# Weight loads on GpSimd's queue, earlier value loads, and the low-rank first half moved inside its pair, in a fused attention and MLP kernel

## The chip, the cores and the metric

The kernel runs on one core of a Trainium2 chip. The metric is device time in microseconds (us), from start to end of one execution. A core has five engines with queues of their own that work in order and wait for one another through semaphores: TensorE (PE, matrix products), VectorE (DVE), ScalarE (ACT), GpSimd (POOL) and SyncE (SP). Here SyncE computes nothing; it starts DMA transfers, each an instruction in its queue. ScalarE and GpSimd can start transfers too.

## The reference

Attention with a sigmoid in place of the softmax, over 4 batches and 12 heads, then two mixing blocks on the joined heads:

```
scores = q @ k.T / sqrt(64) - log(448);  attn = sigmoid(scores);  x = attn @ v     # per head, 448 x 64
h = x.T @ U @ V;  u = x + h.T                                                      # U 448 x 32, V 32 x 448
x = u + relu(u @ w_ch1) @ w_ch2                                                    # 768 -> 3072 -> 768
theta = x @ w_theta;  y = w_tok_r @ (x * cos(theta)) + w_tok_i @ (x * sin(theta))
u = x + y;  out = u + relu(u @ w_ch)
```

The inputs of attention are 32-bit floats; U, V and the weights are 64-bit floats, which the kernel loads as pairs of 32-bit words and turns into 32-bit floats itself. Most factors are split into a rounded high part and the remainder, and a product is taken as hi·hi + hi·lo + lo·hi.

## The kernel before

**Attention** is the first stage. It takes two heads of one batch at a time: 24 pairs, numbered p = 0 to 23, six to a batch. The loop is at lines 614 to 658, and its text is the order of the instructions on every engine. In one pass over p TensorE does the score products of p in three chunks of 128 keys (`QK`, tile `sc`, line 404) and the value products of pair p-1 (`AV`, tile `av`, line 430, and `AV_rest`, line 442). ScalarE turns a chunk of scores into weights (tile `A`, `AL` for the last 64 keys, line 395). VectorE transposes and splits the queries and keys of p+1 (`TK`, `TQ`, `K_lo`). `XN` transposes the finished x of pair p-2 back (tile `xt`, line 454) and VectorE copies it to the tile `xn` (line 455). `xn` has one buffer, so the first copy of a batch must wait until the batch before has been read out of it. The scores have two PSUM buffers: the chunk after the next must wait until ScalarE has read this one.

**The low-rank term.** `U1(b)` multiplies U with the batch's `xn` (tile `p`, line 464, 12 products in the program, 24 rows in the trace), and ScalarE and VectorE split the result into `pc`. `U2_one` (lines 608 to 612, 487) multiplies `pc` by `vcat`, the split of V, and VectorE adds the product `h` to x (line 493). `pc` and `vcat` stack their parts along the 128 rows of the contraction, 32 rows each. U1 for batches 0, 1 and 2 is issued at p = 8, 14 and 20 (lines 644 to 647), and U2 runs twice a pass in the three passes that follow. U1 for batch 3 comes after attention (line 716).

**Loads.** Queries and keys (`load_qk`, four transfers of 56 KB for each tile) are asked for four pairs ahead, values (`load_v`: one of 384 KB and two of 32 KB, for two pairs) at the end of each even pass, for the two pairs from p+2. A value tile has two buffers. All of these are in SyncE's queue, but for pair 0's queries and first values, which ScalarE starts. Each transfer uses one of eight completion semaphores in turn, and an issue waits for the transfer that had the semaphore before, so at most eight are under way in SyncE's queue.

**Converting the 64-bit weights.** A `Conv` job (lines 124 to 162) loads words to a tile `ws` (three buffers, 768 KB for a weight tile), then takes five steps on ScalarE and VectorE, and its first step asks for the load of the job after the next. Nine jobs run inside attention, two steps a pass (`early_step`): w1, U, V for even and odd batches, then six more weight tiles. Their loads are in SyncE's queue where the program text comes to them.

**After attention** come the two large products in 12 blocks of 4 batches (`ch1`, `ch2`), the token mixing and the last product. From the end of the first block's second batch (line 778) `late["sp"]` is set, and the low part of a weight is then made by GpSimd and not by VectorE.

Of the kernel before, what the change touches and what calls it, by code (L numbers as in the profile page):

```python
# [24 lines left out]
def tile_kernel(  # L25
# [156 lines left out]
    def fin_split(dest, key, name, tag):  # L182
        def fin(a, t):
            dest[key] = ring(tag, name)
            split(dest[key], a, lo_dve if late.get("sp") is None else lo_pool)
        return fin

    def load_row(src, r0):
        def dma(s):
            nc.sync.dma_start(out=s.rearrange("p n t -> p (n t)"), in_=src[r0:r0 + P, :])  # L190
        return dma

    def conv_w1(i, j):
        c0 = (i * FB + j) * P

        def dma(s):
            nc.sync.dma_start(
                out=s.rearrange("p (k f) t -> p k (f t)", k=NK),
                in_=w1_w[:, 2 * c0:2 * (c0 + P)].rearrange("(k p) f -> p k f", p=P),
            )  # L200
        return Conv(f"w1_{i}_{j}", P, DM, dma, fin_split(w1_t, (i, j), f"w1_{i}_{j}", "w1"))
# [69 lines left out]
    def conv_U():  # L271
        def dma(s):
            sv = s.rearrange("p (a c r) t -> p a c (r t)", a=2, c=NC)

            def put(o, i):
                nc.sync.dma_start(out=o, in_=i)

            for par in range(2):
                for c0, n0, n1 in ((0, 0, P), (1, P, NFULL * P), (NFULL, S - P, S)):
                    for n, t, m in runs(par, n0, n1):  # L280
                        if m > P:
                            put(sv[:, par, c0:NFULL], U_w[t:t + m, :].rearrange("(c p) w -> p c w", p=P))
                        else:
                            put(sv[n - n0:n - n0 + m, par, c0], U_w[t:t + m, :])

        def dest():
            return u_in.rearrange("p a c r -> p (a c r)").bitcast(U32)
        return Conv("U", P, 2 * NC * R, dma, None, dest=dest)

    def conv_V(par):  # L290
        def dma(s):
            sv = s.rearrange("r n t -> r (n t)")
            for n, t, m in runs(par, 0, S):
                nc.sync.dma_start(out=sv[:, 2 * n:2 * (n + m)], in_=V_w[:, 2 * t:2 * (t + m)])

        def fin(a, t):
            o = vcat[:, par]
            for g in (0, 2):
                hi_act(o[g * R:(g + 1) * R], a)
                lo_dve(o[(g + 1) * R:(g + 2) * R], a, o[:R])  # L300
        return Conv(f"V{par}", R, S, dma, fin)
# [11 lines left out]
    u_in = ap.tile([P, 2, NC, R], F32, name="u_in")  # L313
    vcat = ap.tile([P, 2, S], F32R, name="vcat")

# [143 lines left out]
    def U1(b, p):  # L459
        ps = ps_a.tile([P, 512], F32, tag="ux", name=f"p1_{b}")  # L460
        for c in range(NC):
            r = slice(P - REM if c == NFULL else 0, P)
            for g in range(3):
# [3 lines left out]
                )  # L467
        o = p.tile([P, DM], F32R, tag="pc", name=f"pc_{b}")
        for g in range(3):
# [7 lines left out]
    def u1_lo():  # L477

        while u1_t:
            ps, o = u1_t.pop()  # L480
            for g in range(3):
                x = ps[g * R:(g + 1) * R, :2 * P]
                sl = slice(2 * g * P, 2 * (g + 1) * P)
                for m in range(2):
                    lo_dve(o[(2 + m) * R:(3 + m) * R, sl], x, o[:R, sl])

# [127 lines left out]
    for p in range(NP):  # L614
# [13 lines left out]
        if nx:  # L628
            K_lo(p + 1)
        U2_one(p, 0)  # L630
        QK(p, 2)
# [10 lines left out]
        if p % 2:  # L642
            AV_rest(p // 2)
        b, r = divmod(p - 2 - NH, NH)
        if b >= 0 and r == 0:
            U1(b, ap)
        u1_lo()
        U2_one(p, 1)
        if p in (4, 6):
            early_step()  # L650
        if p + 4 < NP:
            load_qk(p + 4)
        if p % 2 == 0 and p + 2 < NP:
            load_v(p // 2 + 1)
        if p == 0:
# [53 lines left out]
    uv, uv_st = pool("uv", "right")  # L709
    vlast = uv.tile([P, S], F32R, name="vlast")  # L710
    split_u(1, u01, 0, NK, lo_pool, lo_dve)
# [293 lines left out]
```

## Time and profile before

| | |
|---|---|
| median of 3 runs | 1198.64 us (1196.73 to 1199.26) |
| the profiled execution's own time | 1195.74 us |
| its span, first to last instruction | 1194.0 us |
| busy, PE / DVE / ACT / POOL | 1173.7 / 651.2 / 366.2 / 155.7 us |
| weight loads `ws_w`, median from issue to landing | 4.5 us for 768 KB |
| `k` and `q` loads on SyncE, the same | 2.5 and 2.3 us for 56 KB |

Attention ends at about 184 us. The busy times are shares of the whole span; what a wait costs is read from the stage in which it lies. Matrix products overlap, so a product's own length is not its cost: the distance between starts is. The chain of waits gives such distances for TensorE while it is the engine that ends last. An instruction's bracket in the timeline says how long its engine was idle before it and what ended that.

### The profile page before, as it was taken

The page shows a single profiled execution, that of the slowest core. Times are in us where ns is not written, and L with a number is a line of the kernel's source. Part 1 is how long each engine was busy: PE and PEld are TensorE (multiplying, and loading weights), DVE is VectorE, ACT ScalarE, POOL GpSimd, SP SyncE. Part 2 cuts the span into 40 slices and gives each one's busy share as a digit, 9 for nine tenths or more (in the row PEclk, how much of TensorE's full clock was granted, in tenths as well). Part 3 has the DMA queues.
Part 4 walks back from the last instruction along what each step waited for, and adds up shares of the span by engine and source line. Part 5 has one row for each costly group of instructions (what it writes and reads, how often), then busy time and mean ns, then how long its engine had stood idle before and what let it go on. Part 6 is the DMA issues. An engine that isn't in the chain of part 4 may idle for free.

```text
span 1194.0 us, 15048 instructions
## 1 busy us (share of the span) xinstructions
PE 1173.7 (98%) x6172; PEld 1005.7 (84%) x6172; DVE 651.2 (55%) x828; ACT 366.2 (31%) x482; POOL 155.7 (13%) x94
## 2 busy tenths in 40 slices
PE   8899989999999999999999999999999999999998
PEld 4434437999999999999999999999989999999997
DVE  5676865455555555555546565656454642833443
ACT  6667665211122211221212121212124431631110
POOL 0000001411111111111111111212002421320000
PEclk9999999999999999999999999999999999999999
DMA  7687630011222122212222241415242000040344
GB/s 140 143 162 163 116 90 1 27 53 54 84 95 96 53 84 95 95 56 82 95 95 73 75 148 54 159 53 185 110 157 80 1 1 1 3 158 1 52 65 69
DMA packets 177988, 99.18 MB, mean 83 GB/s; under 512 B 140064, under 2 KB 170048, under 8 KB 177792
## 3 DMA queue, kind: packets, MB, share of 16 engines
q1 hardware_dynamic: 152976, 94.79, 28.0%
q10 hardware_dynamic: 24944, 3.44, 2.0%
q8 instruction: 48, 0.79, 0.3%
q14 instruction: 20, 0.16, 0.0%
HBM read 80.05 MB, written 18.15 MB: 82 GB/s over the span
## 4 chain that ended last, share of the span: by engine, by line
PE 94%; DMA 2%; DVE 1%; SPq 1%; issue 0%; ACT 0%; ACTq 0%; DVEq 0%
PE y L698 10%; PE g L676 10%; PE y L700 10%; PE g L678 10%; PE g L677 10%; PE y L699 10%; PE av L430 4%; PE sc L404 3%; PE y L887 3%; PE y L888 3%; PE y L886 3%; PE th L809 2%; PE th L813 2%; PE th L810 2%; PE wc L968 2%; PE wc L969 2%
## 5 line engine op out<-in xcount | busy, mean ns | idle before, releaser
L702 DVE TENSOR_TENSOR X<-y,X 128x896 f32<-128x896 f32 x144 | 157.1, 1091 | 113.3 <-PE y L700 111.8
L698 PE MATMUL y<-gh,w 128*128 128x448 f32 x576 | 211.6, 367 | 0.0
L676 PE MATMUL g<-uh,w 128*128 128x448 f32 x576 | 211.1, 367 | 0.0
L677 PE MATMUL g<-ul,w 128*128 128x448 f32 x576 | 210.9, 366 | 0.0
L700 PE MATMUL y<-gh,w 128*128 128x448 f32 x576 | 210.9, 366 | 0.0
L678 PE MATMUL g<-uh,w 128*128 128x448 f32 x576 | 210.9, 366 | 0.0
L699 PE MATMUL y<-gl,w 128*128 128x448 f32 x576 | 210.8, 366 | 0.0
L683 ACT ACTIVATE gh<-g 128x896 fp32r<-128x896 f32 x48 | 44.1, 919 | 414.9 <-PE g L678 414.9
L684 DVE SCALAR_TENSOR_TENSOR gl<-g,gh 128x896 fp32r<-128x896 f32 x48 | 52.4, 1091 | 190.7 <-ACT gh L683 190.7
L112 POOL TENSOR_TENSOR w<-ca_w,w 128x768 fp32r<-128x768 f32 x42 | 77.8, 1853 | 497.0 <-ACT w L109 497.0
L676 PEld LDWEIGHTS g<-uh,w 128*128 128x128 f32 x576 | 108.2, 188 | 9.7 <-issue 0.4
L698 PEld LDWEIGHTS y<-gh,w 128*128 128x128 f32 x576 | 108.2, 188 | 9.6 <-issue 0.4
L700 PEld LDWEIGHTS y<-gh,w 128*128 128x128 f32 x576 | 108.2, 188 | 9.5
L678 PEld LDWEIGHTS g<-uh,w 128*128 128x128 f32 x576 | 108.2, 188 | 9.4
L677 PEld LDWEIGHTS g<-ul,w 128*128 128x128 f32 x576 | 108.2, 188 | 9.2
L699 PEld LDWEIGHTS y<-gl,w 128*128 128x128 f32 x576 | 108.2, 188 | 9.1
L395 ACT ACTIVATE A<-sc,bias_s 128x896 f32<-128x896 f32 x72 | 69.8, 1004 | 22.9 <-PE sc L404 22.6
L430 PE MATMUL av<-A,v 128*64 128x448 f32 x288 | 65.5, 563 | 4.1 <-DMA v<-in_v_dram 4.1
L886 PE MATMUL y<-tok,zh 128*128 128x448 f32 x168 | 61.7, 367 | 0.0
L887 PE MATMUL y<-tok,zh 128*128 128x448 f32 x168 | 61.5, 366 | 0.0
L888 PE MATMUL y<-tok,zl 128*128 128x448 f32 x168 | 61.4, 366 | 0.0
L109 ACT ACTIVATE w<-ca_w 128x768 fp32r<-128x768 f32 x48 | 40.3, 839 | 63.8 <-PE y L700 63.8
(132 smaller groups left out, 1619.1 us busy)
## 6 DMA issues: line engine op xcount, KB each, us to landing
ws_w<-in_moe_w_ch_dram SPq DMA_DIRECT2D x48, 768.0 KB, 4.5
k<-in_k_dram SPq DMA_DIRECT2D x96, 56.0 KB, 2.5
q<-in_q_dram SPq DMA_DIRECT2D x92, 56.0 KB, 2.3
ws_th<-in_moe_w_theta_dram SPq DMA_DIRECT2D x6, 768.0 KB, 4.2
th_d<-sp_th SPq DMA_DIRECT2D x6, 768.0 KB, 4.2
ws_wc<-in_moe_w_ch_dram SPq DMA_DIRECT2D x6, 768.0 KB, 4.7
wc_d<-sp_wc SPq DMA_DIRECT2D x6, 768.0 KB, 4.1
th_r<-th_d SPq DMA_DIRECT2D x6, 768.0 KB, 5.3
```

The costliest lines, as they stand in the source:

```text
L112: nc.gpsimd.tensor_sub(o, a, b)
L430: nc.tensor.matmul(ps[h * D:(h + 1) * D, :S], v_t[p // 2][:, 2 * (p % 2) + h, c, :], A_t[p, c][:, h, :], start=c == 0 and p % 2 == 0, stop ...
L676: nc.tensor.matmul(o, wh[:, sl], uh_t[b][:, kk, :], start=kk == 0, stop=False)
L677: nc.tensor.matmul(o, wh[:, sl], ul_t[b][:, kk, :], start=False, stop=False)
L678: nc.tensor.matmul(o, wl[:, sl], uh_t[b][:, kk, :], start=False, stop=kk == NK - 1)
L698: nc.tensor.matmul(o, wh[:, sl], gh[:, j, :], start=j == 0, stop=False)
L699: nc.tensor.matmul(o, wh[:, sl], gl[:, j, :], start=False, stop=False)
L700: nc.tensor.matmul(o, wl[:, sl], gh[:, j, :], start=False, stop=j == FB - 1)
L702: nc.vector.tensor_add(x, ps[:, :, :S], x)
L886: nc.tensor.matmul(o, zh[:, sl], tok_h[:, i, :], start=n == 0, stop=False)
L887: nc.tensor.matmul(o, zh[:, sl], tok_l[:, i, :], start=False, stop=False)
L888: nc.tensor.matmul(o, zl[:, sl], tok_h[:, i, :], start=False, stop=n == NZ - 1)
```

## The change

All loads of `Conv` jobs inside attention (weights, U, V) are issued by GpSimd in place of SyncE; after line 778's point they are on SyncE as before. `load_v` stands ahead of `load_qk` at the end of an even pass. `U1` and `u1_lo` move from the end of passes 8, 14 and 20 into their middle, between `K_lo` and the first `U2_one`. `pc` and `vcat` lose their fourth 32 rows: the contraction runs over hi·hi, lo·hi and hi·lo (96 rows) and no longer over lo·lo, and for each batch VectorE makes three low parts of `pc` in place of six, and for each of two V tiles one low part in place of two.

```diff
--- before.py
+++ after.py
@@ -182,19 +182,22 @@
     def fin_split(dest, key, name, tag):
         def fin(a, t):
             dest[key] = ring(tag, name)
-            split(dest[key], a, lo_dve if late.get("sp") is None else lo_pool)
+            split(dest[key], a, lo_pool if "sp" in late else lo_dve)
         return fin
+
+    def loader():
+        return nc.sync if "sp" in late else nc.gpsimd
 
     def load_row(src, r0):
         def dma(s):
-            nc.sync.dma_start(out=s.rearrange("p n t -> p (n t)"), in_=src[r0:r0 + P, :])
+            loader().dma_start(out=s.rearrange("p n t -> p (n t)"), in_=src[r0:r0 + P, :])
         return dma
 
     def conv_w1(i, j):
         c0 = (i * FB + j) * P
 
         def dma(s):
-            nc.sync.dma_start(
+            loader().dma_start(
                 out=s.rearrange("p (k f) t -> p k (f t)", k=NK),
                 in_=w1_w[:, 2 * c0:2 * (c0 + P)].rearrange("(k p) f -> p k f", p=P),
             )
@@ -273,7 +276,7 @@
             sv = s.rearrange("p (a c r) t -> p a c (r t)", a=2, c=NC)
 
             def put(o, i):
-                nc.sync.dma_start(out=o, in_=i)
+                nc.gpsimd.dma_start(out=o, in_=i)
 
             for par in range(2):
                 for c0, n0, n1 in ((0, 0, P), (1, P, NFULL * P), (NFULL, S - P, S)):
@@ -291,13 +294,13 @@
         def dma(s):
             sv = s.rearrange("r n t -> r (n t)")
             for n, t, m in runs(par, 0, S):
-                nc.sync.dma_start(out=sv[:, 2 * n:2 * (n + m)], in_=V_w[:, 2 * t:2 * (t + m)])
+                nc.gpsimd.dma_start(out=sv[:, 2 * n:2 * (n + m)], in_=V_w[:, 2 * t:2 * (t + m)])
 
         def fin(a, t):
             o = vcat[:, par]
             for g in (0, 2):
                 hi_act(o[g * R:(g + 1) * R], a)
-                lo_dve(o[(g + 1) * R:(g + 2) * R], a, o[:R])
+            lo_dve(o[R:2 * R], a, o[:R])
         return Conv(f"V{par}", R, S, dma, fin)
 
     cv, cv_st = pool("cv")
@@ -311,7 +314,7 @@
     ps_a, ps_a_st = pool("ps_a", "left", PSUM)
     ps_b, ps_b_st = pool("ps_b", "right", PSUM)
     u_in = ap.tile([P, 2, NC, R], F32, name="u_in")
-    vcat = ap.tile([P, 2, S], F32R, name="vcat")
+    vcat = ap.tile([3 * R, 2, S], F32R, name="vcat")
 
     vl_t, AL_t = {}, {}
     q_t, k_t, v_t, qq_t, kk_t, A_t, av_t, xn_t = {}, {}, {}, {}, {}, {}, {}, {}
@@ -465,7 +468,7 @@
                     ps[g * R:(g + 1) * R, :2 * P], u_in[r, b % 2, c, :], xn_t[b][r, c, 2 * g * P:2 * (g + 1) * P],
                     start=c == 0, stop=c == NC - 1,
                 )
-        o = p.tile([P, DM], F32R, tag="pc", name=f"pc_{b}")
+        o = p.tile([3 * R, DM], F32R, tag="pc", name=f"pc_{b}")
         for g in range(3):
             x = ps[g * R:(g + 1) * R, :2 * P]
             sl = slice(2 * g * P, 2 * (g + 1) * P)
@@ -481,8 +484,7 @@
             for g in range(3):
                 x = ps[g * R:(g + 1) * R, :2 * P]
                 sl = slice(2 * g * P, 2 * (g + 1) * P)
-                for m in range(2):
-                    lo_dve(o[(2 + m) * R:(3 + m) * R, sl], x, o[:R, sl])
+                lo_dve(o[2 * R:, sl], x, o[:R, sl])
 
     def U2(b, d, ps, vc, n=1):
         for m in range(n):
@@ -627,6 +629,10 @@
             early_step()
         if nx:
             K_lo(p + 1)
+        b, r = divmod(p - 2 - NH, NH)
+        if b >= 0 and r == 0:
+            U1(b, ap)
+            u1_lo()
         U2_one(p, 0)
         QK(p, 2)
         if not nx:
@@ -641,17 +647,13 @@
             AV(p - 1, 2)
         if p % 2:
             AV_rest(p // 2)
-        b, r = divmod(p - 2 - NH, NH)
-        if b >= 0 and r == 0:
-            U1(b, ap)
-        u1_lo()
         U2_one(p, 1)
         if p in (4, 6):
             early_step()
+        if p % 2 == 0 and p + 2 < NP:
+            load_v(p // 2 + 1)
         if p + 4 < NP:
             load_qk(p + 4)
-        if p % 2 == 0 and p + 2 < NP:
-            load_v(p // 2 + 1)
         if p == 0:
             seq[1].load()
         if p:
@@ -707,7 +709,7 @@
         AV(NP - 1, c)
     ap1_st.close()
     uv, uv_st = pool("uv", "right")
-    vlast = uv.tile([P, S], F32R, name="vlast")
+    vlast = uv.tile([3 * R, S], F32R, name="vlast")
     split_u(1, u01, 0, NK, lo_pool, lo_dve)
     XN(NP - 2)
     ch1(0, 0)
```

SyncE's queue from pair 2's queries on. First before, then now; the first number in a name is the pair (`k_3`) or the pair of passes (`v_1` holds the values of pairs 2 and 3).

```order
L327 DMA q_2_127<-in_q_dram 32x14x32 x4
L197 DMA ws_w1_0_0_136<-in_moe_w_ch1_dram 128x6x256
L327 DMA k_3_138<-in_k_dram 32x14x32 x4
L327 DMA q_3_139<-in_q_dram 32x14x32 x4
L327 DMA k_4_243<-in_k_dram 32x14x32 x4
L327 DMA q_4_244<-in_q_dram 32x14x32 x4
L349 DMA v_1_253<-in_v_dram 128x4x192
L354 DMA vl_1_254<-in_v_dram 64x2x64 x2
L276 DMA ws_U_258<-in_moe_U_dram 128x64
L276 DMA ws_U_258<-in_moe_U_dram 128x2x64
L276 DMA ws_U_258<-in_moe_U_dram 128x64
L276 DMA ws_U_258<-in_moe_U_dram 64x64 x2
```

```order
L330 DMA q_2_127<-in_q_dram 32x14x32 x4
L330 DMA k_3_138<-in_k_dram 32x14x32 x4
L330 DMA q_3_139<-in_q_dram 32x14x32 x4
L352 DMA v_1_243<-in_v_dram 128x4x192
L357 DMA vl_1_244<-in_v_dram 64x2x64 x2
L330 DMA k_4_248<-in_k_dram 32x14x32 x4
L330 DMA q_4_249<-in_q_dram 32x14x32 x4
L330 DMA k_5_322<-in_k_dram 32x14x32 x4
L330 DMA q_5_323<-in_q_dram 32x14x32 x4
L352 DMA v_2_394<-in_v_dram 128x4x192
L357 DMA vl_2_395<-in_v_dram 64x2x64 x2
L330 DMA k_6_399<-in_k_dram 32x14x32 x4
```

The weight load behind `q_2` and the U loads are gone, and each `v` stands ahead of two query and key tiles that it stood behind. On GpSimd, which before did nothing between making the identity and its first subtraction after attention, the weight load of the first job is now the next instruction behind the identity, with U and V behind it:

```order
masks.py:197 MEMSET ident_63 128x128
masks.py:199 ISA
masks.py:199 AFFINE_SELECT ident_63<-ident_63 128x128
L200 DMA ws_w1_0_0_136<-in_moe_w_ch1_dram 128x6x256
L279 DMA ws_U_258<-in_moe_U_dram 128x64
L279 DMA ws_U_258<-in_moe_U_dram 128x2x64
L279 DMA ws_U_258<-in_moe_U_dram 128x64
L279 DMA ws_U_258<-in_moe_U_dram 64x64 x2
L279 DMA ws_U_258<-in_moe_U_dram 128x2x64
L279 DMA ws_U_258<-in_moe_U_dram 128x64
L297 DMA ws_V0_300<-in_moe_V_dram 32x896
```

ScalarE in pass 8 and the beginning of pass 9, before and now:

```order
L395 ACTIVATE A_8_0_799<-sc_8_0_792,bias_s_64 128x896
L395 ACTIVATE A_8_1_808<-sc_8_1_801,bias_s_64 128x896
L109 ACTIVATE kh_9_823<-kT_9_810 128x384
L395 ACTIVATE A_8_2_835<-sc_8_2_828,bias_s_64 128x896
L395 ACTIVATE AL_4_849<-sl_4_844,bias_s_64 128x896
L109 ACTIVATE X_66<-av_7_777 128x448
L109 ACTIVATE pc_0_867<-p1_0_854 32x256 x6
L395 ACTIVATE A_9_0_903<-sc_9_0_896,bias_s_64 128x896
L395 ACTIVATE A_9_1_912<-sc_9_1_905,bias_s_64 128x896
```

```order
L398 ACTIVATE A_8_0_798<-sc_8_0_791,bias_s_64 128x896
L398 ACTIVATE A_8_1_807<-sc_8_1_800,bias_s_64 128x896
L109 ACTIVATE kh_9_822<-kT_9_809 128x384
L109 ACTIVATE pc_0_840<-p1_0_827 32x256 x6
L398 ACTIVATE A_8_2_857<-sc_8_2_850,bias_s_64 128x896
L398 ACTIVATE AL_4_871<-sl_4_866,bias_s_64 128x896
L109 ACTIVATE X_66<-av_7_776 128x448
L398 ACTIVATE A_9_0_899<-sc_9_0_892,bias_s_64 128x896
L398 ACTIVATE A_9_1_908<-sc_9_1_901,bias_s_64 128x896
```

The six copies of `pc_0` moved ahead of two of the pass's weight computations, `A_8_2` and `AL_4`.

VectorE at the same place, before and now:

```order
L118 TENSOR_TENSOR kl_9_824<-kT_9_810,kh_9_823 128x384
L455 COPY xn_1_837<-xt_6_838 128x4x128
L118 TENSOR_TENSOR pc_0_867<-p1_0_854,pc_0_867 32x256 x6
L156 SCALAR_TENSOR_TENSOR ca_V1_755<-ca_V1_755,ws_V1_481 32x448
L377 STREAM_TRANSPOSE kT_10_914<-k_10_699 128x448
```

```order
L118 TENSOR_TENSOR kl_9_823<-kT_9_809,kh_9_822 128x384
L118 TENSOR_TENSOR pc_0_840<-p1_0_827,pc_0_840 32x256 x3
L458 COPY xn_1_859<-xt_6_860 128x4x128
L156 SCALAR_TENSOR_TENSOR ca_V1_754<-ca_V1_754,ws_V1_481 32x448
L380 STREAM_TRANSPOSE kT_10_910<-k_10_704 128x448
```

The copy to `xn_1`, which reuses the buffer that U1 reads, stood ahead of the six subtractions of `pc_0` and stands now behind three.

## Rows read from the trace of the kernel before

**Rows 1.** The page, its first line.

```profile
span 1194.0 us, 15048 instructions
```

**Rows 2.** The stretches view; per engine us busy (instructions), then clock, DMA share, GB/s.

```profile
184.00:1000.00 816.00, 815.91 (x4097) 750.04 (x4096) 444.87 (x474) 197.26 (x255) 136.71 (x78) 1.00 0.23 79
```

**Rows 3.** The chain that ended last, around 150 us; start us, us, what.

```profile
133.05 0.41 PE h L489
...
148.25 1.66 PE av L430 x8
...
154.54 1.65 PE av L430 x8
...
159.40 2.02 PE p L464 x24
```

**Rows 4.** The timeline, TensorE alone; start, length, instruction, count, [idle before, releaser].

```profile
28.08 1.72 PE L430 MATMUL av<-A,v 128*64 128x448 f32 x8 [0.94 <-DMA v<-in_v_dram]
...
43.89 1.72 PE L430 MATMUL av<-A,v 128*64 128x448 f32 x8 [3.17 <-DMA v<-in_v_dram]
```

**Rows 5.** The chain again, around the three low-rank first halves.

```profile
62.83 1.65 PE av L430 x8
...
82.10 1.65 PE av L430 x8
...
108.86 1.66 PE av L430 x8
...
127.78 1.65 PE av L430 x8
...
173.65 1.65 PE av L430 x8
```

**Rows 6.** The timeline of all engines, pairs 8 and 9.

```profile
62.31 1.90 ACT L395 ACTIVATE A<-sc,bias_s 128x896 f32<-128x896 f32 x2 [0.31 <-PE sc L404]
...
64.41 0.47 PE L404 MATMUL sc<-qh,kh 64*128 64x448 f32 x2
...
67.61 2.06 PE L464 MATMUL p<-xn,u_in 128*32 128x256 f32 x24
...
69.73 2.32 ACT L109 ACTIVATE pc<-p 32x256 fp32r<-32x256 f32 x6 [1.44 <-PE p L464]
69.73 0.69 DVE L455 COPY xn<-xt 128x512 f32<-128x512 f32 x1 [4.20 <-PE p L464]
...
72.08 2.59 DVE L118 TENSOR_TENSOR pc<-p,pc 32x256 fp32r<-32x256 f32 x6 [1.66 <-ACT pc L109]
...
76.57 1.76 PE L430 MATMUL av<-A,v 128*64 128x448 f32 x4
```

**Rows 7.** The stretches view, after the first low-rank first half.

```profile
69.50:84.00 14.50, 12.26 (x68) 5.13 (x65) 12.31 (x25) 10.69 (x17) 0.00 (x0) 0.88 0.80 152
```

**Rows 8.** The timeline of SyncE's queue, 16 to 41 us.

```profile
16.05 4.04 SPq L327 DMA_DIRECT2D q<-in_q_dram  x4
...
22.28 1.99 SPq L327 DMA_DIRECT2D q<-in_q_dram  x4
24.31 0.48 SPq L349 DMA_DIRECT2D v<-in_v_dram  x1
...
26.26 3.90 SPq L276 DMA_DIRECT2D ws_U<-in_moe_U_dram  x7
...
40.11 0.43 SPq L349 DMA_DIRECT2D v<-in_v_dram  x1
```

**Rows 9.** The stretches view, 10 to 14 us.

```profile
10.00:14.00 4.00, 3.65 (x20) 1.43 (x20) 3.06 (x6) 3.57 (x5) 0.00 (x0) 1.00 0.69 112
```

**Rows 10.** The page, ScalarE's DMA queue: packets, MB, share of 16 engines.

```profile
q10 hardware_dynamic: 24944, 3.44, 2.0%
```

**Rows 11.** The waits view, GpSimd: total us, times, longest.

```profile
POOL ul L112 <- ACT uh L109: 211.9, 3, 188.7
```

**Rows 12.** The timeline, the first score product.

```profile
7.68 0.47 PE L404 MATMUL sc<-qh,kh 64*128 64x448 f32 x2 [0.48 <-ACT qh L109]
```

## The prediction

> **What bounds the kernel now.** I read the page's first line, then the stretches, then the chain of waits inside attention, and last the timelines around the places where the chain leaves TensorE.
>
> The span is 1194.0 us [rows 1] and the execution took 1195.74, so 1.74 us lie around it. From 184 to 1000 us TensorE is busy for 815.91 of 816.00 us at full clock, with the DMA engines at a share of 0.23 [rows 2]. The reader is to see that nothing waits there: whatever attention ends sooner, the kernel ends sooner. All parts of the change lie before that, apart from batch 3's three fewer subtractions, which stand beside a full TensorE.
>
> In attention the chain says what a pass costs when nothing stalls. The value products of successive passes start at 148.25 and 154.54, that is 6.29 us, with nothing but TensorE between them; one product `h` adds 0.41, two of them in a pass with U2 (I use 0.40 each, so 7.09), and a U1 adds 2.02 [rows 3]. So a pass of 6.29 is TensorE's own work, and longer ones show stalls. There are two kinds.
>
> The first kind is values that come late. TensorE stands idle for 0.94 us before 28.08 and for 3.17 us before 43.89, both ended by the `v` transfer [rows 4]. Together 4.1 us.
>
> The second kind is U1. Two passes from the value products before a U1 should take 6.29 + 2.02 + 7.09 = 15.40 us, where the U1 falls into them. They take 82.10 - 62.83 = 19.27, 127.78 - 108.86 = 18.92 and 173.65 - 154.54 = 19.11 [rows 3, 5], so U1 loses 3.87, 3.52 and 3.71, in sum 11.1 us. The timeline says why. U1 starts at 67.61, behind everything else of its pass. VectorE's copy to `xn` was held 4.20 us, until U1 had read the one `xn` buffer; ScalarE's six `pc` parts took from 69.73 to 72.05 and VectorE's six another 2.59 [rows 6]. The first `h` needs all of them and stands in the middle of the next pass, and VectorE's transposes for the pass after that queue behind. In the 14.5 us that follow, the granted clock averages 0.88 of full speed, that is part of the time at the lower of the two levels, 1.2 in place of 2.4 GHz; four value products take 1.76 us there [rows 6, 7]. That loss is inside the 3.87 and goes with the gap.
>
> **U1 in mid-pass.** No instruction of TensorE is added or removed. In pass 8 U1 would come before the chunk at 64.41 [rows 6], so from 64.41 to 66.43. The `pc` parts are then ready before the next pass's middle: ScalarE 66.5 to 68.8, VectorE's three low parts (2.59 / 6 = 0.43 each, one high part ahead) to about 69.3. The first `h` comes at about 73, so its wait goes whole. The `xn` copy no longer finds U1 in front, since U1 has read the buffer before the pass's own transposes. What is late next is ScalarE: the 2.32 us of `pc` stand ahead of `A_8_2` and `AL_4`, which start at 68.9 and take 0.95 each at the pace of two in 1.90 [rows 6], so they end at 69.8 and 70.8. TensorE has 3.20 us of work from the third chunk to the pass's end (64.41 to 67.61, where U1 stood), so it arrives at 69.63. Its next chunk needs the PSUM buffer that `A_8_2` frees at 69.8, and the one after it, ready at 70.3, the buffer that `AL_4` frees at 70.8. I take 0.7 us for each U1. Bounds: 0, if `pc` fits beside the work, and 2.32, if all of ScalarE's six parts end up on the path. Three times: 2.1 us, 0 to 7.0. A gain beyond the 11.1 is excluded, since these passes would then beat TensorE's own work.
>
> **Values sooner.** SyncE loses the weight load and the seven U loads (3.90 us of its queue), and `v_1` no longer waits for two tiles of 1.99 us each [rows 8]. The value load that left at 24.31 leaves at about 20 or earlier, which covers the 0.94. The one that left at 40.11 gains 3.90 + 2 x 2 = 7.9 us, against the 3.17. The last reader of the buffer it needs is in pass 2, long before. Behind the value load `k_4` and `q_4` come up to 1.95 us later (24.31 to 26.26), less what the weight load took; they are two passes early in the rest of the loop, and in the worst case one of them costs those 1.95, which I keep in the range. I take the whole 4.1 as gained.
>
> **The issue on GpSimd.** Its cost has no row, but GpSimd waits 188.7 us in one piece for the first subtraction after attention [rows 11], and all 18 new transfers but none of its work fall into that time. A load is asked for two jobs, ten steps, ahead, which is five passes or 31 us; the longest wait for a transfer in the rows is 3.17 us [rows 4]. So I put it at nothing, bounds 0 and those 3.17 once. If that cover failed, ScalarE's first step of a job would hold `A` behind it.
>
> **The first weight load at the start.** Here the change costs. The weights now leave behind GpSimd's making of the identity, before the first queries and keys have landed, and run beside them. ScalarE's queue, nearly all 128-byte pieces, moved 3.44 MB in 2.0% of 16 engines' 1194 us, which is 144 GB/s [rows 10]; large pieces go at 79 / 0.23 = 343 GB/s [rows 2]. So 768 KB take 2.3 us of all engines, U (two sets of 512 rows of 256 bytes) at most 1.8 and V 0.3: 4.4 us at worst. From 10 to 14 us the share is 0.69, so 1.2 us are spare before the second pair's queries are in [rows 9]. The nearest row: when the same weight load went just ahead of `k_3` and `q_3`, the four issues of `q_3` took 4.04 us in place of 1.99 [rows 8], a loss of 2.0. To it I add what U and V leave over, 2.1 - 1.2 = 0.9, halved as they come only behind the weights and SyncE's eight transfers in flight leave gaps: 2.5 us, bounds 0 and 4.4. A gain is excluded: nothing in front of the first three pairs' loads goes away.
>
> The Trainium skill (DMA: Bandwidth & Descriptors, "Queues, rings and completion order") says that a DMA engine goes round between the queues that have work, one packet each. By that rule the weights' larger pieces take more than an equal share, the cost is the upper end and the sum 1188.0 + 1.9 = 1189.9, where the row of `q_3` gives 1188.0. The trace of before, in which one queue carried nearly all, can't show it.
>
> **The rest.** Three fewer subtractions a batch and one fewer for each V tile shorten VectorE's queue only; they count in the U1 term. A contraction over 96 rows in place of 128 streams the same 448 columns; no row shows 96. I take no change; bounds are a quarter of the 0.41 gained or lost, the share of rows that goes, for 18 products in attention 1.8 us.
>
> **The sum.** Gained 11.1 + 4.1 = 15.2; given back 2.1 + 2.5 = 4.6; net 10.6 us. Against the profiled execution 1195.74 - 10.6 = 1185.1. The median of the runs is 2.90 above that execution; I carry this over: 1198.64 - 10.6 = 1188.0. With the bounds: 1183.4 (nothing given back) to 1194.8 (7.0 + 4.4 given back).
>
> **Rivals.**
>
> A, the start is hidden and U1 fits: `pc` is read in ScalarE's slack and the transfers fill gaps. For it: ScalarE was busy for only 10.69 of 14.5 us [rows 7]. Against: the row of the slow `q_3`. Time 1183.4.
>
> B, both costs in full: the weights' pieces of 1 KB get the engines ahead of the 128-byte ones (4.4 us), and all of `pc` lands on the path (7.0). For it: the 4.04 us; against: the 1.2 us to spare and that ScalarE catches up in the next pass. 15.2 - 11.4 = 3.8 gained, 1194.8.
>
> C, values don't come sooner, because SyncE's queue waits elsewhere (its eight semaphores): only U1 is gained. 10.6 - 4.1 = 6.5, so 1192.1. Against it: the 3.90 us of U that go.
>
> D, slower. SyncE has eight transfers in flight, and a pass needs 9.5 (eight for queries and keys, three for values every other pass). A pass then takes at least 9.5 / 8 of the mean time from issue to landing. If GpSimd's queue, running ahead and unthrottled by SyncE, stretches this time, queries and keys bound the loop. It binds from 6.29 x 8 / 9.5 = 5.3 us a transfer, and at 5.75 the 24 passes lose 24 x 0.54 = 13, more than the net gain. At 6 us they lose 24 x 0.835 = 20.0: 1188.0 + 20.0 = 1208. For it: `q_3` at twice its issue time beside a weight load [rows 8]. Against it: the bytes are the same as before, and even at a share of 0.80 with a weight load inside, in the stretch from 69.5, the engines were not full [rows 7].
>
> **How the numbers follow.** My forecast holds with 0.62, A 0.14, B 0.12, C 0.05, D 0.07. The forecast's own range is 1184 to 1193. Eight in ten need A and most of B: 1183 to 1195. A measurement of this kernel can tell 0.2%, 2.4 us, from no change. Below 1196.2 lie forecast, A, C and most of B: faster 0.88; a part of B, with a misjudged start, is within 2.4 us: 0.05; slower 0.07, from D.
>
> **What would show it.** Right: in the changed trace the value products of the passes around a U1 are within 1 us of 15.40 in two passes, no `h` waits for `pc`, the `xn` copy does not wait for U1, no value product waits for `v`, and the granted clock is 1.0 after the U1s. The first score product starts later than 7.68 [rows 12], by up to 4. TensorE's steady pass stays 6.29. Wrong: a steady pass above 6.4 (D), a wait for `v` left before the value products (C), two passes around a U1 above 17 (B), first products that start no later than before (A).

## The result and the profile after

The changed kernel took 1186.55 us (median of 4 runs, 1186.13 to 1187.58) against 1198.93 us (4 runs) for the one before, run beside it: ratio 0.9902, 95% interval 0.9885 to 0.9919. The profiled execution took 1186.37 us, with a span of 1184.6.

First the lines of after that answer to [rows 1, 2, 7]: the page's first line, and the stretches view (per engine us busy and instructions, then clock, DMA share, GB/s) from 174 us on and behind the first U1.

```profile
span 1184.6 us, 15058 instructions
```

```profile
69.50:84.00 14.50, 14.21 (x89) 6.36 (x88) 11.43 (x23) 11.75 (x17) 0.55 (x1) 1.00 0.82 163
...
174.00:990.00 816.00, 815.91 (x4098) 750.17 (x4098) 443.57 (x470) 197.71 (x255) 136.76 (x78) 1.00 0.23 79
```

Behind attention nothing changed: the same 816 us hold 4098 products where they held 4097. Behind U1 TensorE is busy for 14.21 of 14.5 us and not 12.26, at clock 1.00 and not 0.88. So the gain lies in attention. It is best read from the starts of the value products, one group of eight a pass: the last, of pass 23, starts at 171.07 in place of 180.67, 9.6 us sooner. First before, then after: pass 1, the two ends of the two passes around the first U1 (after alone; before's are in [rows 5]), and pass 23.

```profile
14.88 1.72 PE L430 MATMUL av<-A,v 128*64 128x448 f32 x8
...
180.67 1.72 PE L430 MATMUL av<-A,v 128*64 128x448 f32 x8
```

```profile
19.18 1.72 PE L433 MATMUL av<-A,v 128*64 128x448 f32 x8
...
62.59 1.72 PE L433 MATMUL av<-A,v 128*64 128x448 f32 x8
...
78.54 1.72 PE L433 MATMUL av<-A,v 128*64 128x448 f32 x8
...
171.07 1.72 PE L433 MATMUL av<-A,v 128*64 128x448 f32 x8
```

Pass by pass, before and after:

| where | before | after | gained |
|---|---|---|---|
| value products of pass 1 | 14.88 | 19.18 | -4.30 |
| interval to pass 2 | 5.91 | 5.69 | 0.22 |
| interval to pass 3 (value wait before) | 7.29 | 6.29 | 1.00 |
| interval to pass 5 (value wait before) | 9.52 | 6.28 | 3.24 |
| two passes from U1 of batch 0 | 19.27 | 15.95 | 3.32 |
| the same, batch 1 | 18.92 | 15.94 | 2.98 |
| the same, batch 2 | 19.11 | 15.95 | 3.16 |

They come to 9.6: start -4.30, pass 2 0.22, values 4.24, U1 9.46. The passes that are not in the table take the same to 0.01 us.

The start. The chain that ended last, then GpSimd's instructions, then TensorE's first score product (timeline; in the bracket how long the engine stood idle and what ended that):

```profile
3.90 7.54 DMA k<-in_k_dram
```

```profile
1.46 0.98 POOL L200 DMA_DIRECT2D ws_w<-in_moe_w_ch_dram  x1
2.44 4.12 POOL L279 DMA_DIRECT2D ws_U<-in_moe_U_dram  x7
8.65 0.52 POOL L297 DMA_DIRECT2D ws_V<-in_moe_V_dram  x1 [2.10 <-DMA ws_w<-in_moe_w_ch_dram]
```

```profile
11.58 0.47 PE L407 MATMUL sc<-qh,kh 64*128 64x448 f32 x2 [3.85 <-ACT qh L109]
```

The weights and U are asked for from 1.46 to 6.56, on top of the first keys. One transfer of keys is under way for 7.54 us, whose median is 2.4 in the whole kernel. The first score product waits 3.85 us for what comes of it and starts at 11.58, not at 7.68 [rows 12]. The other 0.40 of the 4.30 lies between the first score product and the value products: 7.60 us, where it was 7.20. The stretches there (the DMA share adds up the time of all packets under way, so it can pass 1):

```profile
5.00:6.00 1.00, 1.00 (x7) 1.00 (x6) 0.00 (x0) 0.00 (x0) 1.00 (x2) 1.00 0.99 342
6.00:10.00 4.00, 1.73 (x16) 1.49 (x14) 0.34 (x1) 0.00 (x0) 1.07 (x3) 1.00 1.24 205
10.00:14.00 4.00, 2.12 (x12) 1.38 (x12) 2.03 (x4) 2.01 (x3) 0.00 (x0) 0.85 1.21 198
14.00:18.00 4.00, 3.89 (x22) 1.72 (x20) 2.98 (x6) 3.39 (x5) 0.00 (x0) 0.73 0.69 108
```

From 5 to 6 us the engines move 342 GB/s, what they moved with large pieces in [rows 2]. After the 3.85 us in which TensorE stood, its granted clock averages 0.85 and 0.73 of full speed, so part of the time it ran at 1.2 and not 2.4 GHz; before, it was 1.00 from 10 to 14 [rows 9]. How much of the 0.40 the lower clock cost, no run parts from the rest.

The page also shows that GpSimd's loads are in a queue of another kind than SyncE's (q1), here with its packets, MB and share of 16 engines:

```profile
q1 hardware_dynamic: 147984, 88.01, 26.5%
q0 software_dynamic: 1728, 6.78, 1.8%
```

That is 3.9 KB a packet. SyncE's queue had 152976 packets and 94.79 MB before, so the same 6.78 MB took 4992 packets there, 1.4 KB each. The change made these packets larger too, beside sending them earlier; no run parts the two.

U1 in pass 8, in the timeline of all engines, which answers to [rows 6]:

```profile
64.25 2.06 PE L467 MATMUL p<-xn,u_in 128*32 128x256 f32 x24
...
66.36 2.31 ACT L109 ACTIVATE pc<-p 32x256 fp32r<-32x256 f32 x6 [1.66 <-PE p L467]
...
68.70 1.01 ACT L398 ACTIVATE A<-sc,bias_s 128x896 f32<-128x896 f32 x1
68.70 1.28 DVE L118 TENSOR_TENSOR pc<-p,pc 32x256 fp32r<-32x256 f32 x3 [1.95 <-ACT pc L109]
...
69.60 1.00 ACT L398 ACTIVATE AL<-sl,bias_s 128x896 f32<-128x896 f32 x1
...
69.75 0.47 PE L407 MATMUL sc<-qh,kh 64*128 64x448 f32 x2 [0.25 <-ACT A L398]
...
70.02 0.69 DVE L458 COPY xn<-xt 128x512 f32<-128x512 f32 x1
...
73.10 0.47 PE L491 MATMUL h<-vcat,pc 96*128 96x448 f32 x1
```

`pc` is ready at 69.98, three microseconds before `h` reads it; the copy to `xn` has no bracket, where it waited 4.20 us for U1; what is left is ScalarE, whose six `pc` parts stand ahead of `A`: TensorE waits 0.25 for that. `h` over 96 rows costs what it cost over 128: passes with two of them take 7.09 to 7.10 us before and after. TensorE's waits in attention, as a list (total, times, longest), confirm it:

```profile
PE sc L407 <- ACT qh L109: 3.8, 1, 3.8
PE warm L590 <- POOL ident masks.py:199: 1.4, 1, 1.4
PE sc L407 <- ACT A L398: 0.7, 3, 0.2
PE sc L407 <- DVE ql L118: 0.3, 1, 0.3
```

No wait for `v` is left [rows 4]. In SyncE's queue the values that left at 24.31 and 40.11 [rows 8] leave at 22.90 and 33.73:

```profile
22.90 0.48 SPq L352 DMA_DIRECT2D v<-in_v_dram  x1
...
33.73 0.42 SPq L352 DMA_DIRECT2D v<-in_v_dram  x1
```

### The profile page after: what moved, and what is told of

Its sections match the earlier page's. It is cut to its first block, busy times and chain, and to the rows that moved or that the text cites. A ratio compares the mean times of both kernels' runs of the same rounds, so it can differ in the third digit from the quotient of the medians.

```text
span 1184.6 us, 15058 instructions
## 1 busy us (share of the span) xinstructions
PE 1172.4 (99%) x6172; PEld 1005.9 (85%) x6172; DVE 644.7 (54%) x814; ACT 365.7 (31%) x482; POOL 167.2 (14%) x112
## 3 DMA queue, kind: packets, MB, share of 16 engines
q0 software_dynamic: 1728, 6.78, 1.8%
## 4 chain that ended last, share of the span: by engine, by line
PE 97%; DMA 1%; ACT 1%; SPq 0%; issue 0%; DVE 0%; DVEq 0%
PE y L700 10%; PE g L678 10%; PE g L679 10%; PE y L702 10%; PE g L680 10%; PE y L701 10%; PE av L433 5%; PE sc L407 4%; PE y L889 3%; PE y L890 3%; PE y L888 3%; PE th L811 2%; PE th L815 2%; PE th L812 2%; PE wc L970 2%; PE wc L971 2%
```

## The experiments

Each is the changed kernel with the edit shown. "Starts" are again those of the value products.

**All loads back on SyncE.**

```diff
-        return nc.sync if "sp" in late else nc.gpsimd
+        return nc.sync
```

and the same for U and V.

> The changed kernel with all weight, U and V loads back in SyncE's queue; U1 in mid-pass, three terms and earlier values are kept. Theory (the start is late because the first weight load and U run beside the first queries and keys, and the values come in time without SyncE being relieved): the first score product is back at 7.7 us instead of 11.6, no value product waits for v, the value products of pass 23 start about 4 us sooner, so about 1182.5 us against 1186.55 for the changed kernel. Rival (the values are in time only because SyncE lost the weights): the start is 4 us sooner, but waits for v of 1 to 4 us come back in passes 3 and 5, so 1184 to 1187. Second rival (the start is late for another reason, such as the order of the first transfers on SyncE): first score product at 11.6 as in the changed kernel, 1186 or more.

Measured: 1185.44 us (1184.83 to 1186.12), ratio 0.99 (0.9887 to 0.9914). Pass 1 starts at 14.63, so the late start comes from sending these loads from GpSimd at the very beginning. No value waits here either. But the rows behind the weights are late again: the interval to pass 2 is 6.82 and that to pass 5 is 8.14, where after has 5.69 and 6.28. The timeline shows the second, with the keys of pair 5 behind U in SyncE's queue:

```profile
35.69 0.65 DVE L380 STREAM_TRANSPOSE kT<-k 128x448 f32<-128x448 f32 x1 [2.73 <-DMA k<-in_k_dram]
...
38.92 0.97 PE L416 MATMUL sl<-qT,kT 64*64 64x448 f32 x4 [0.90 <-DVE qT L365]
```

Pass 23 starts at 169.77, 1.3 us before after's. So the move to GpSimd's queue paid 4.55 at the start and got 3.25 back later; in these profiles it lost 1.3 us by itself, which the ratios, 0.990 in both, neither confirm nor deny. The theory had the start and the values right, and missed the time by 3 us through the late keys; the time is in the first rival's range, but not for its reason.

**Values behind queries and keys again.**

```diff
-        if p % 2 == 0 and p + 2 < NP:
-            load_v(p // 2 + 1)
         if p + 4 < NP:
             load_qk(p + 4)
+        if p % 2 == 0 and p + 2 < NP:
+            load_v(p // 2 + 1)
```

> The changed kernel with load_qk ahead of load_v again. Theory (either of the two, an emptier queue or the earlier place, is enough to bring the values in time, since SyncE without U and the weights is passes ahead): no value product waits for v for more than 0.5 us, 1186 to 1187.5 us. Rival (the earlier place is what counts): the wait of about 1 us before pass 3's value products and part of the 3.2 us before pass 5's are back, 1188 to 1191 us.

Measured: 1187.28 us (1187.1 to 1187.57), ratio 0.9916 (0.9902 to 0.9929). TensorE waits for no `v`. From pass 2 on the intervals are those of after; only the start is 0.75 later, in one profile of each. So once SyncE has lost the weights and U, the earlier place of `load_v` isn't needed; and with the earlier place, the run before this one shows, values are in time with the weights on SyncE too.

**U1 at the end of its pass, three terms kept.**

```diff
-        b, r = divmod(p - 2 - NH, NH)
-        if b >= 0 and r == 0:
-            U1(b, ap)
-            u1_lo()
         U2_one(p, 0)
 ...
             AV_rest(p // 2)
+        b, r = divmod(p - 2 - NH, NH)
+        if b >= 0 and r == 0:
+            U1(b, ap)
+        u1_lo()
```

> The changed kernel with U1 and its low parts back at the end of passes 8, 14 and 20, three terms kept. Theory (U1's place makes the loss, because the xn copy stands behind U1 and the first h comes half a pass after it): the three stretches of two passes around U1 are 18 to 19.3 us again instead of 15.95, together 7 to 9.5 us, so 1193.5 to 1196 us; the three fewer subtractions spare at most 1.3 us of each stall. Rival (the three terms, by half the low parts, are what removed the stall): 16 to 17 us a stretch, 1187 to 1190 us.

Measured: 1191.99 us (1190.19 to 1193.45), ratio 0.9954 (0.9939 to 0.997). The three two-pass stretches take 17.35, 16.52 and 17.82 us. The time lies between the two expectations. The waits of TensorE in attention name what is left:

```profile
PE h L491 <- DVE X L495: 2.7, 2, 1.6
PE h L491 <- DVE pc L118: 2.4, 3, 0.8
```

`h` still waits for `pc`, for 2.4 us and no longer for 6.2, and VectorE's later steps are late behind it.

**Four terms, U1 in mid-pass.**

```diff
-                lo_dve(o[2 * R:, sl], x, o[:R, sl])
+                for m in range(2):
+                    lo_dve(o[(2 + m) * R:(3 + m) * R, sl], x, o[:R, sl])
```

and 128 rows for `pc` and `vcat`, with two low parts for each V tile.

> The changed kernel with the fourth 32 rows of pc and vcat back (six low parts of pc and two of each V tile on VectorE), U1 in mid-pass. Run e3 left the split open: with U1 back at the end the three U1 stretches took 17.35, 16.52 and 17.82 us against 15.95 each in the changed kernel and 19.3, 18.9 and 19.1 before, so the place bought 3.8 us and the shorter split (with the emptier queues) the other 5.6. Theory 1 (either alone nearly closes the gap, since from mid-pass there are 3.8 us between the last high part of pc and the first h, and six low parts need 2.6): stretches at 15.9 to 16.3, total within 1 us of the changed kernel, 1186 to 1188 us. Rival (the parts add up): stretches at 17 to 18, 1190 to 1192 us.

Measured: 1188.06 us (1187.44 to 1188.37), ratio 0.9924 (0.9908 to 0.9941). Stretches 16.53, 15.96 and 16.42. In sum over the three: 57.30 before, and with the emptied queue of SyncE 51.69 with three terms alone, 48.91 with the place alone, 47.84 with both. Of the 9.46 us either alone recovers more than half; together they overlap. With U1 in mid-pass, the removal of the fourth 32 rows is worth 1.07 us. Two of the stretches lie up to 0.2 us above the first theory's range, the time just at its end. No run has the place or the split alone with SyncE's queue as it was before, so what the emptied queue gave to U1 is not parted from them.

**The first weight load held back until the second pair's keys are there.** GpSimd makes a small subtraction of `kT_1` ahead of the load, so that its queue waits.

```diff
+    gate = cpool.tile([P, 1], F32, name="gate")
 ...
-    seq[0].load()
 ...
+        if p == 0:
+            nc.gpsimd.tensor_sub(gate, kT_t[1][:, :1], kT_t[1][:, :1])
+            seq[0].load()
```

> The changed kernel, but GpSimd first subtracts one column of the second pair's transposed keys from itself, so that the first weight load, U and V are issued only when the first two key tiles and the first queries are there (about 10 us). Theory (the late start is the company of these loads): first score product at 7.7 instead of 11.6 us, pass 1's value products at about 15 instead of 19.2, up to 1 us lost when the first weights come a little later than ScalarE wants them: 1182 to 1183.5 us, faster than both kernels. Rival (the contention only moves on, to the queries of pairs 2 and 3): start at 7.7, but 2 to 4 us more of waits for queries in passes 1 to 3: 1185 to 1187 us.

Measured: 1191.67 us (1191.17 to 1191.91), ratio 0.9952 (0.994 to 0.9965), where both expectations had it faster than the changed kernel or level with it. Attention did what it should: pass 1 starts at 13.94 and pass 23 at 167.44, 3.63 before after. What was lost lies behind attention, where neither the gate nor a load of it runs. The stretches view there, first of this kernel, then of after:

```profile
400.00:700.00 300.00, 300.00 (x1472) 273.91 (x1471) 164.40 (x176) 61.48 (x77) 39.36 (x21) 1.00 0.27 87
```

```profile
400.00:700.00 300.00, 300.00 (x1488) 277.24 (x1487) 166.15 (x177) 63.31 (x80) 39.40 (x22) 1.00 0.28 91
```

TensorE is full in both, at full clock, and does 1472 products where after does 1488. The next two kernels part the gate from the new tile.

**The same gate, written to a tile that was there already** (`warm` for `gate`, no new tile).

> Run e5 again, but GpSimd's first subtraction writes to the existing tile warm, so that no tile is added and every address on chip is that of the changed kernel. In e5 pass 23 came 3.6 us sooner than in the changed kernel, and then the matrix products after attention ran about 1% slower with TensorE full (735 for 746 in 250 to 400 us). Theory (the added 4-byte tile moved the weights and operands behind it): TensorE's rate after attention is that of the changed kernel, 746 products in 250 to 400, and the 3.6 us arrive at the end, 1182 to 1183.5 us. Rival (the later weight loads or the subtraction itself slow what follows): 1191 us again.

Measured: 1183.67 us (1183.24 to 1183.82), ratio 0.9888 (0.9868 to 0.9908); 746 and 1489 products in the two stretches. Pass 1 starts at 14.86, as before the change, and pass 23 at 167.93. The interval to pass 2 is 6.86, since the weights now meet the queries of pair 3:

```profile
18.34 0.65 DVE L365 STREAM_TRANSPOSE qT<-q 128x448 f32<-128x448 f32 x1 [4.20 <-DMA q<-in_q_dram]
```

**Only an unused tile, no gate.**

```diff
     X = cpool.tile([P, NK, NT], F32, name="X")
+    pad = cpool.tile([P, 1], F32, name="pad")
```

> The changed kernel with nothing but an unused tile of 4 bytes a partition added behind X, which moves the tiles behind it. Theory (addresses): attention as in the changed kernel, products after it about 1% slower, 1194 to 1196 us. Rival: 1186.5 us, no change.

Measured: 1194.65 us (12 runs, 1194.0 to 1195.67), ratio 0.9975 (0.9963 to 0.9987); 736 and 1471 products. So the tile alone costs 8 us, two thirds of the 12.4 by which the medians of before and after differ. It takes 32 bytes of each partition, and every tile allocated behind it on its side moves by as much. The change itself moves none: all tiles of after lie where they lay before.

**Two more lengths of it,** 64 and 128 bytes (`[P, 16]` and `[P, 32]`).

> The changed kernel with an unused tile of 64 bytes a partition behind X, where the earlier one took 32. Theory: what slowed the products after attention is where their operands start within 64 bytes; these starts are as in the changed kernel again, so 746 products in 250:400, 1488 in 400:700, and 1186.5 us. Rival: any move of the tiles slows them (by which tiles come to lie beside each other, or by distance); about 736 and 1471 products, and 1194 us.

> The changed kernel with an unused tile of 128 bytes a partition behind X, after 32 and 64. With 64 the products ran between the two rates (1480 in 400:700, against 1488 and 1471), so the place within 64 bytes does not decide alone. Theory: the place within 128 bytes decides; it is restored here, so 746 products in 250:400, 1488 in 400:700 and 1186.5 us. Rival: the distance between the tiles that move (weights and gh, gl) and those that do not (uh0, ul0, tok, X) counts, or the address as a whole; then some other rate, 1480 products or fewer, and 1189 us or more.

| moved by | products 250:400 | 400:700 | median us (runs) | ratio, interval |
|---|---|---|---|---|
| 0 (after) | 746 | 1488 | 1186.55 (4) | 0.9902, 0.9885 to 0.9919 |
| 32 bytes | 736 | 1471 | 1194.65 (12) | 0.9975, 0.9963 to 0.9987 |
| 64 bytes | 737 | 1480 | 1189.18 (6) | 0.9925, 0.9907 to 0.9942 |
| 128 bytes | 743 | 1487 | 1186.57 (4) | 0.9897, 0.9881 to 0.9914 |

The theory of 64 bytes fell: the time lies between. That of 128 bytes fits the time, and in these two stretches the products to three. But from 700 to 1000 us there are 1535 products where after has 1523 (and 1521 and 1531 with 32 and 64), so the rates are not after's: time lost early is won back late, and the equal sum is partly luck. The last section has the rates. Which operand it is, the weights, `gh` and `gl` that move or `uh0`, `ul0`, `uh1`, `ul1` and `tok` on the other side that don't, stays open.

**Gating U to a later pass too,** on top of that gate, and the first conversion step at the end of pass 1.

```diff
-        if p == 0:
+        if p == 1:
+            nc.gpsimd.tensor_sub(warm, kT_t[2][:, :1], kT_t[2][:, :1])
             seq[1].load()
```

> Run e9 with two more edits: GpSimd issues the U load only when the third pair's keys are transposed (pass 1), and pass 1's first conversion step is left to its end, so that ScalarE does not wait for the first weights. In e5 pass 2 came 7.40 us after pass 1 instead of 5.69, behind the weights and U beside the fourth pair's queries. Theory: that 1.7 us shrinks to under 0.7, first score product at 7.7, total 1 us under e9, 1181 to 1182.5 us. Rival (the weight load alone holds the queries up, whatever U does): as e9, 1182 to 1183.5.

Measured: 1183.97 us (1183.65 to 1184.21), ratio 0.989 (0.987 to 0.991). No gain, and a little above the rival's range: the interval to pass 2 is 7.95. VectorE waits 5.09 us for `q_3`, and the score product behind it another 1.45 for the conversion step on ScalarE, which now stands ahead of it. U leaves at 14.79 in place of 12.04 but still before `q_3` lands, so this run doesn't tell whether the weight load alone holds the queries up.

**The gate in pass 2, behind `kT_3`.**

```diff
-    seq[0].load()
 ...
+        if p == 2:
+            nc.gpsimd.tensor_sub(warm, kT_t[3][:, :1], kT_t[3][:, :1])
+            seq[0].load()
```

with U at the end of pass 2 and conversion from pass 3.

> The weight load, U and V wait here for kT_3 (pass 2) rather than for kT_1, through the tile warm that is there already; U's load and the conversion of the weights move back with it. Theory: what holds pass 2 up in the gated kernel (6.86 us from the first value product of pass 1 to that of pass 2) is the weight load beside q_3; without it the pass takes the 5.7 of the changed kernel, so about 1.1 us less: 1182.5 us. Rival: the weights meet the rows of passes 3 to 5 instead, one of these intervals grows by 1 us or more over the changed kernel's 6.3, and the time is that of the first gated kernel, 1183.7, or above.

Measured: 1182.74 us (1182.01 to 1183.57), ratio 0.9871 (0.9849 to 0.9893). The starts of passes 1 to 4:

```profile
14.63 1.72 PE L433 MATMUL av<-A,v 128*64 128x448 f32 x8
...
20.32 1.72 PE L433 MATMUL av<-A,v 128*64 128x448 f32 x8
...
26.60 1.72 PE L433 MATMUL av<-A,v 128*64 128x448 f32 x8
...
33.94 1.72 PE L433 MATMUL av<-A,v 128*64 128x448 f32 x8
```

The theory's pass 2 came, 5.69; and the rival's loss came in pass 4, 7.34 in place of 6.29. Pass 23 is 0.36 before the first gated kernel's. This version beats both kernels: 1182.01 to 1183.57 us against 1186.13 to 1187.58 for after (in another set of runs; the medians of before beside them are 1199.16 and 1198.93). Over the first gated kernel, 1183.24 to 1183.82, the gain isn't certain.

**And half of `pc`'s high copies on VectorE,** on top of the late gate.

```diff
-            for m in range(2):
-                hi_act(o[m * R:(m + 1) * R, sl], x)
+            hi_act(o[:R, sl], x)
+            nc.vector.tensor_copy(o[R:2 * R, sl], x)
```

> As the late gate, and the second high copy of pc in a block's first half goes to VectorE instead of ScalarE, so that ScalarE's A of the next pass comes sooner. Theory: what is left of the first half's stall is the wait for ScalarE's A (three waits of sc, 0.7 us in all, and what follows them); it goes, each of the three stretches falls from 15.95 by 0.3 to 0.5, and the time is 1 to 1.4 us under the late gate's. Rival: VectorE, which has three steps of 1.28 us on pc there already, gets late with xn or qT, and the time is that of the late gate or above it.

Measured: 1183.09 us (1182.7 to 1185.78), ratio 0.9881 (0.986 to 0.9901), no gain. Each U1 stretch does fall, from 15.95 to 15.73, by less than expected. TensorE's waits show why: the three of 0.2 for `A` are gone, one of 0.5 in another pass is not; and in pass 4 the queries come later still (0.64 for `qh`, where it was 0.25). VectorE's three steps on `pc`, named in the rival, take 1.28 us together.

```profile
PE sc L407 <- DVE qh L369: 0.6, 1, 0.6
PE sc L407 <- ACT A L398: 0.5, 1, 0.5
```

## Why the prediction was right, and where its terms were off

**The mechanism held.** TensorE bounds the kernel and attention is where it waits. Both kinds of stall went as the steps said, the start paid for it, the steady pass stayed 6.29, and what attention won stayed won: 9.6 us there, 9.4 in the profiled executions.

**U1 in mid-pass: right, in cause and size.** 9.46 us against 9.0. The first `h` no longer waits for `pc`, the copy to `xn` no longer for U1, the clock is back at 1.00. What is late next is ScalarE, as forecast: 0.55 for each U1 where I took 0.7, and in pass 8 at the two chunks that the step named, those at 69.75 and 70.66. With half of ScalarE's copies moved to VectorE 0.22 of the 0.55 went; that the rest is ScalarE's too is not shown. The step counted the place of U1 and the three fewer low parts together; apart, the place alone recovers 8.4 us and the shorter split alone 5.6, each with the emptied queue.

**Values sooner: right in size, with more than it needed.** 4.24 against 4.1. The step named SyncE's lighter queue and the new place of `load_v` together; no value waits without the new place, and none with the weights back on SyncE, so either alone does it. The 1.95 us that I feared for `k_4` and `q_4` did not come. The two value loads left 1.4 and 6.4 us sooner, where I had 4.3 and 7.9, since SyncE's first eight issues took 9.54 us in place of 5.61.

**The start: mis-sized.** The term was 2.5, between 0 and 4.4; measured 4.30, nearly the upper bound. The step that failed is "the nearest row": `q_3` beside one weight load in a queue that already had a lead. At the start there is no lead, and the first keys wait; the gate bears this out, since behind the second pair's keys the same loads cost 1.17. The sum 2.3 + 1.8 + 0.3 of bytes at full rate came nearer, but by luck in part: 342 GB/s were moved from 5 to 6 us, and only 205 and 198 from there to 14. Nor is 4.4 a bound, and 4.30 is one profile. Six more kernels here start with the same loads, and their pass 1 begins between 17.77 and 20.24, so 2.9 to 5.4 us late; of the seven, four lie above 4.4 and none at 2.5. Inside the 4.30 are the 0.40 between the first score product and the value products, which no step had.

The Trainium skill's rule (DMA: Bandwidth & Descriptors, "Queues, rings and completion order"), that an engine goes round between queues a packet at a time, had also given the upper end. The 4.30 us lie there; in what order an engine took the packets, no run here shows.

**GpSimd's issue: free where I looked.** Among ScalarE's seven longest waits in attention, down to 0.9 us, none is for a weight. But by its own test the move of the loads lost 1.3 us in the profiles: 4.55 lost at the start, 3.25 won later.

**The median agrees better than the terms do.** Net in attention I forecast 10.6 and 9.6 came. I then carried over the 2.90 us by which the median of before lay above its profiled execution; after's median lies 0.18 above its own. 1188.0 + 1.0 for the terms, + 0.2 for what lies around attention, - 2.7 for the offset is the measured 1186.5. That the offset's miss and the terms' nearly cancel is luck. The profiled executions alone compare as 1185.1 forecast and 1186.37 measured.

**The rivals.** A needed an early start, C a wait for `v`, D a steady pass over 6.4: none is in the trace. B's start came nearly in full, but not its U1 (1.65 us against 7.0).

## What to carry to other kernels

A load that is moved to an idle queue to unload a busy one also loses the delay that the busy queue gave it: hold it back on purpose, by something that the transfers it would collide with have to finish first, and place it where the rows ahead have slack. Here the same load cost 4.3 us at the start and 1.1 to 1.2 in pass 2 or 4. And compare kernels only after counting the work per microsecond in a stretch that neither changes: an unused tile of four bytes cost 8.1 us of the 12.4 that the medians had won.

## What the runs showed of the hardware that was not expected

TensorE runs the same products at more than one rate, with its clock at 1.00 and no idle time, and where the tiles lie has a part in which. One batch of `ch1` or of `ch2` is 36 products (`g` or `y`), and from the first product of one such group to the first of the next it is 7.30 or 7.44 us, 0.203 or 0.207 for a product (with moved tiles 7.36 too). First after, then the kernel with the unused tile of 32 bytes, then that of 128:

```profile
220.20 0.37 PE L678 MATMUL g<-uh,w 128*128 128x448 f32 x1
...
227.50 0.36 PE L700 MATMUL y<-gh,w 128*128 128x448 f32 x1
...
687.64 0.55 PE L264 MATMUL tkt<-ident,sp_tok 112*128 112x112 f32 x4
...
705.40 0.37 PE L678 MATMUL g<-uh,w 128*128 128x448 f32 x1
...
712.84 0.37 PE L700 MATMUL y<-gh,w 128*128 128x448 f32 x1
```

```profile
218.96 0.37 PE L679 MATMUL g<-uh,w 128*128 128x448 f32 x1
...
226.40 0.37 PE L701 MATMUL y<-gh,w 128*128 128x448 f32 x1
```

```profile
220.89 0.37 PE L679 MATMUL g<-uh,w 128*128 128x448 f32 x1
...
228.33 0.37 PE L701 MATMUL y<-gh,w 128*128 128x448 f32 x1
...
794.90 0.37 PE L679 MATMUL g<-uh,w 128*128 128x448 f32 x1
...
802.20 0.36 PE L701 MATMUL y<-gh,w 128*128 128x448 f32 x1
```

From 200 us of the span on there are 84 groups that nothing interrupts. Their times, and the time from pass 23's value products to the end of the span:

| moved by | 7.27 to 7.31 us | 7.33 to 7.37 | 7.42 to 7.45 | pass 23 to the end |
|---|---|---|---|---|
| 0 (after; before has the same counts) | 57 | 0 | 27 | 1013.5 us |
| 32 bytes | 5 | 22 | 57 | 1022.7 |
| 64 bytes | 37 | 0 | 47 | 1015.3 |
| 128 bytes | 50 | 22 | 12 | 1013.3 |

All ten traces of kernels whose tiles are not moved have the counts of the first row, and the gated kernel that brought the tile has those of the second. So the place of the tiles does change the rates, and in the same way each time. But it does not set it alone: in after, which moved nothing, 57 of the first 59 groups are fast, and from 687.64 us on, when four small transposes (`tkt`) come in the middle of a group of `y`, products that read the same tiles as those ahead of them are slow, and all later groups with them. In the kernel moved by 32 bytes the same kind of transposes at 335.20 turn the rate the other way, from 7.44 to 7.30 for the next group. What sets the rate stays open.
